# Weight conversions issued one operation at a time, operand reloads in pieces on another queue, and an earlier first output load, in a fused attention, expert and SiLU kernel

## Chip, cores and metric

The kernel runs on one core of a Trainium2 chip. The metric is device time in microseconds (us) from the start to the end of one execution, as the median of several runs. The engines are named as the profile names them: PE multiplies matrices (PEld loads its weights), DVE, ACT and POOL are the vector, scalar and GpSimd engines, and SP only issues DMAs here.

## The reference

Three parts follow each other; only their shapes matter here (8 batches, 8 heads, 576 rows of 64, so 4608 tokens of 512 numbers).

```python
# 1: attention through 32 packed rows per head
p_packed = sm_attn(p, k, v)
x = sm_attn(q, p_packed, p_packed)          # -> (4608, 512)
# 2: one expert of 8 for each token
expert_idx = argmax(normalised(x) @ normalised(expert_emb).T / tau)
out[mask] = gate_w[mask, None] * (relu(x[mask] @ w1[e]) @ w2[e])     # 512 -> 1024 -> 512
# 3: feed forward, with weights that arrive as 64-bit floats
h = out @ w_in                               # 512 -> 2048
y = (h / (1 + exp(-h))) @ w_out              # 2048 -> 512
```

## The kernel before

**Attention** (to about 195 us of the profile) is ordered by a table of start times (`TIMES`) and is not touched.

**The middle stage**, `experts` (195 to 522 us), handles the 8 batches b one after the other. For a batch, `A(m)` for m = 0 to 7 makes the hidden layer: 12 matmuls (L528 to L530), then ACT writes a high part (L533) and DVE the remainder (L537). `Mm` prepares the next batch. Then `Bm(c)` for c = 0 to 3 makes the output columns: 48 matmuls (L602 to L604) that need the high and low part of one block of `w2` (`split_w2`, DVE L575), and `Y` (DVE L613) drains the result. Four PSUM tiles `ps` are used in turn. Beside this, the 64-bit numbers of `w_in` and `w_out` are turned into 32-bit ones: 32 tiles of 512 KB are loaded into two buffers `cin` (`conv_load`), `conv` makes six integer operations of each on DVE (L653 to L658) and the result is stored to `wf_d` (`conv_store`). `todo` and `plan` say how many whole tiles are done after each `Bm(c)`: mostly one, two after `Bm(1)`. The program text sets the order on every engine.

**The last stage**, `ffn`, has two parts. The first (522 to 888 us) makes h and its SiLU in 40 groups. `group(z, g)` takes token block z (512 columns for z = 0 to 3, 256 for z = 4) and weight block g. A group is seven products `Pm` of six matmuls each (L854 to L856), that is 42 matmuls; DVE adds (L847) and ACT applies SiLU (L888); four results go to DRAM (`c_d`, `store`, L898) from a ring `cs` of seven buffers. The seventh product of a group, `last`, runs inside the next group, so a weight operand is free only then. Four calls of `hook(h)` in each group let a list `side` of small jobs run (`later(at, ...)` puts a job there for a time `4 * group + h`). Among these jobs are differences of `w_out` blocks: `o_load` reads two tiles `raw` from `wf_d`, `out_sums` makes four DVE subtractions, `u_store` writes `u_d`. The weight operands (1792 KB each) live in four places TT; the groups of the last sweep (list index 16 to 31 of `order`) need the blocks 4 to 7 again. `t_load` (L1036) reads each back from `t_d` on POOL's queue, right after the group that `next_t` names:

```python
next_t = {19: (4, 0), 20: (5, 1), 21: (6, 2), 23: (7, 3)}
...
        group(z, g)
        if i - 1 in next_t:
            t_load(*next_t[i - 1])
```

The second part (888 us to the end) makes the output in 18 units of seven `product`s with 24 matmuls each (L1142 to L1144). A unit reads four or five pieces of `c_d` (`load_unit`, L1084) into `raws`; `split` makes a high part on ACT (L1113) and a low part on DVE; `drain` adds the products up. The first unit's loads stand before the group with index 30, `t_raw` (the raw weights of two more operands) before group 31 and behind the last one. `x_load` (L1245) brings 7 x 512 KB of `w_out` blocks on POOL's queue at index 29, and `x_build` splits them. `order0` is the order of the seven products in the first unit.

Of the kernel before, what the change touches and what calls it, by code (L numbers as in the profile page):

```python
# [539 lines left out]
def experts(tc, st, sums, R, P, first, ident, a2_d, y_d, g_d, pp_d, w1, w2, win, wout, wf_d, u_d):  # L540
# [106 lines left out]

    def conv(x):
# [4 lines left out]
        DVE.tensor_scalar(out=g, in0=hi, scalar1=-(1 << 31), scalar2=1 << 30, op0=ALU.bitwise_and, op1=ALU.bitwise_or)  # L653
        DVE.tensor_scalar(out=u, in0=hi, scalar1=(1 << 31) - 1, scalar2=None, op0=ALU.bitwise_and)
        DVE.tensor_scalar(out=u.bitcast(F32), in0=u.bitcast(F32), scalar1=EXP_LO, scalar2=EXP_HI, op0=ALU.max, op1=ALU.min)
        DVE.scalar_tensor_tensor(out=g, in0=lo, scalar=29, in1=g, op0=ALU.logical_shift_right, op1=ALU.bitwise_or)
        DVE.tensor_scalar(out=u, in0=u, scalar1=4, scalar2=1, op0=ALU.logical_shift_left, op1=ALU.logical_shift_right)
# [4 lines left out]
        if 7 < i < 16:  # L662
# [9 lines left out]
    def conv_store(x):  # L672
        SP.dma_start(out=wf_d[corder[x]], in_=cout[corder[x]])
# [66 lines left out]
    todo = list(range(32))  # L740
    plan = {(0, 0): 0, (0, 1): 0, **{(b, 1): 2 for b in range(1, 7)}, **{(B - 1, c): 0 for c in range(4)}}
    for b in range(B):
# [27 lines left out]
        for c in range(4):  # L770
# [45 lines left out]
            for x in xs:  # L816
                conv_store(x)


def ffn(tc, st, sums, y_d, wf_d, t_d, c_d, u_d, out):  # L820
# [37 lines left out]
    side, clock = [], [0]  # L858
# [21 lines left out]
    def group(z, g):  # L880
# [208 lines left out]
    order0 = (1, 7, 6, 3, 2, 5, 4)  # L1089
# [56 lines left out]
    def drain(s):  # L1146
# [655 lines left out]
```

## Time and profile before

| what | value |
|---|---|
| median of 3 runs (lowest to highest) | 1269.62 us (1269.46 to 1269.73) |
| the profiled execution's own time | 1268.04 us |
| its span, first to last instruction | 1265.6 us |
| busy: PE, PEld, DVE, ACT, POOL | 1202.6 (95%), 1090.8 (86%), 853.7 (67%), 522.4 (41%), 92.6 us (7%) |
| mean granted clock of TensorE | 0.990 |
| DMA | 256.79 MB, mean 203 GB/s |

The profile is one execution; its time lies 1.58 us below the median of the three runs, and 2.4 us of it lie outside the span. PE is busy for most of the span, so what another engine does costs time only where PE stands idle or runs at a lower clock. In the rows further down, `x<-p,x` means that a tile x is written from tiles p and x, and `<-` behind a wait names what ended it.

### The profile page before, as it was taken

The page shows a single profiled execution, that of the slowest core. Times are in us where ns is not written, and L with a number is a line of the kernel's source. Part 1 is how long each engine was busy: PE and PEld are TensorE (multiplying, and loading weights), DVE is VectorE, ACT ScalarE, POOL GpSimd, SP SyncE. Part 2 cuts the span into 40 slices and gives each one's busy share as a digit, 9 for nine tenths or more (in the row PEclk, how much of TensorE's full clock was granted, in tenths as well). Part 3 has the DMA queues.
Part 4 walks back from the last instruction along what each step waited for, and adds up shares of the span by engine and source line. Part 5 has one row for each costly group of instructions (what it writes and reads, how often), then busy time and mean ns, then how long its engine had stood idle before and what let it go on. Part 6 is the DMA issues. An engine that isn't in the chain of part 4 may idle for free.

```text
span 1265.6 us, 25188 instructions
## 1 busy us (share of the span) xinstructions
PE 1202.6 (95%) x10016; PEld 1090.8 (86%) x10017; DVE 853.7 (67%) x1477; ACT 522.4 (41%) x898; POOL 92.6 (7%) x180
## 2 busy tenths in 40 slices
PE   6899988999999998999999999799799999999998
PEld 4677677999988998878788878689799999999998
DVE  3566567678987884687767676347766567777775
ACT  2666653332333233364444344235533334333332
POOL 3133220002001011100000000001000000000000
PEclk9999999999999999999999999899899999999999
DMA  7888738579877944575866545877864645545351
GB/s 195 246 231 226 240 124 266 189 236 335 272 234 236 328 139 157 193 231 188 323 251 232 200 167 169 320 251 241 234 175 133 182 135 134 144 113 159 99 154 34
DMA packets 249914, 256.79 MB, mean 203 GB/s; under 512 B 34872, under 2 KB 196664, under 8 KB 248768
## 3 DMA queue, kind: packets, MB, share of 16 engines
q1 hardware_dynamic: 241680, 239.40, 60.1%
q0 software_dynamic: 1584, 11.01, 2.5%
q10 hardware_dynamic: 6528, 4.72, 1.2%
q8 instruction: 80, 1.31, 0.4%
q14 instruction: 42, 0.34, 0.1%
HBM read 165.30 MB, written 89.78 MB: 202 GB/s over the span
## 4 chain that ended last, share of the span: by engine, by line
PE 50%; DVE 5%; DMA 4%; issue 2%; ACT 1%; SPq 0%; DVEq 0%; ACTq 0%
PE p L1144 9%; PE p L1143 9%; PE p L1142 9%; PE p L854 6%; PE p L855 6%; PE p L856 6%; DVE x L847 2%; DMA c_d<-x 2%; DMA raw<-wf_d 1%; DVE raw L847 1%; PE ps L604 1%; PE ps L602 1%; PE ps L603 1%; PE ps L528 0%; PE ps L530 0%
## 5 line engine op out<-in xcount | busy, mean ns | idle before, releaser
L888 ACT ACTIVATE x<-x 128x512 f32<-128x512 f32 (+1 forms) x111 | 66.5, 603 | 151.2 <-DVE x L847 148.8
L847 DVE TENSOR_TENSOR x<-p,x 128x512 f32<-128x512 f32 (+1 forms) x132 | 83.4, 643 | 55.8 <-PE p L856 42.7
L604 PE MATMUL ps<-hkm,w2s 128*128 128x288 f32 x384 | 113.7, 296 | 2.7 <-DVE w2s L575 2.7
L602 PE MATMUL ps<-hkm,w2s 128*128 128x288 f32 x384 | 114.9, 299 | 1.2 <-DVE yb L613 1.2
L1142 PE MATMUL p<-x,x 128*128 128x256 f32 x380 | 108.5, 286 | 0.0
L1143 PE MATMUL p<-x,x 128*128 128x256 f32 x380 | 108.4, 285 | 0.0
L603 PE MATMUL ps<-hqm,w2s 128*128 128x288 f32 x320 | 94.2, 294 | 0.0
L602 PEld LDWEIGHTS ps<-hkm,w2s 128*128 128x128 f32 x384 | 72.3, 188 | 8.1 <-DVE hqm L537 4.2
L604 PEld LDWEIGHTS ps<-hkm,w2s 128*128 128x128 f32 x384 | 72.3, 188 | 3.5 <-DVE w2s L575 3.4
L1142 PEld LDWEIGHTS p<-x,x 128*128 128x128 f32 x380 | 74.0, 195 | 0.0
L1143 PEld LDWEIGHTS p<-x,x 128*128 128x128 f32 x380 | 73.9, 195 | 0.0
L1144 PE MATMUL p<-x,x 128*128 128x256 f32 x256 | 73.2, 286 | 0.0
L528 PE MATMUL ps<-at,mh 128*128 128x288 f32 x224 | 66.9, 299 | 5.4 <-PEq L692 3.8
L1144 PE MATMUL p<-x,e 128*128 128x256 f32 x248 | 70.2, 283 | 0.0
L530 PE MATMUL ps<-at,mh 128*128 128x288 f32 x224 | 66.9, 298 | 0.0
L529 PE MATMUL ps<-at,mh 128*128 128x288 f32 x224 | 66.8, 298 | 0.0
L533 ACT ACTIVATE hkm<-ps 128x576 fp32r<-128x576 f32 x42 | 27.1, 650 | 84.9 <-PE ps L530 84.9
L574 ACT CAST w2s<-w2c 128x1024 fp32r<-128x1024 f32 x32 | 33.7, 1054 | 66.7 <-PE ps L603 32.3
L603 PEld LDWEIGHTS ps<-hqm,w2s 128*128 128x128 f32 x320 | 60.0, 188 | 0.0
L847 DVE TENSOR_TENSOR x<-p,y 128x512 f32<-128x512 f32 (+1 forms) x57 | 33.2, 582 | 39.1 <-PE p L856 31.7
L847 DVE TENSOR_TENSOR x<-x,x 128x512 f32<-128x512 f32 (+2 forms) x58 | 49.5, 853 | 14.4 <-ACT x L1113 11.5
L1152 ACT COPY y<-p 128x256 f32<-128x256 f32 x18 | 6.7, 372 | 126.4 <-PE p L1144 126.4
(425 smaller groups left out, 3857.8 us busy)
## 6 DMA issues: line engine op xcount, KB each, us to landing
c_d<-x SPq DMA_DIRECT2D x144, 256.0 KB, 2.3
raww1c<-c_d SPq DMA_DIRECT2D x36, 512.0 KB, 6.8
rawe<-c_d SPq DMA_DIRECT2D x36, 512.0 KB, 7.0
w1c<-in_moe_w_dram SPq DMA_DIRECT2D x32, 512.0 KB, 6.5
w2c<-in_moe_w_dram SPq DMA_DIRECT2D x32, 512.0 KB, 6.9
y_d<-yb SPq DMA_DIRECT2D x36, 288.0 KB, 5.0
raw<-y_d SPq DMA_DIRECT2D x36, 256.0 KB, 4.0
vm<-in_v_dram SPq DMA_DIRECT2D x8, 1024.0 KB, 10.3
```

What stands on the lines that cost most here:

```text
L528: PE.matmul(out=a[:, i, 0:H2], lhsT=mh[0][:, t, f], rhs=at[0][:, t, n], start=t == 0, stop=False)
L530: PE.matmul(out=a[:, i, 0:H2], lhsT=mh[1][:, t, f], rhs=at[0][:, t, n], start=False, stop=t == 1)
L602: PE.matmul(out=a[:, i, 0:H2], lhsT=h[:, k, :], rhs=hT(0, k, n), start=k == 0, stop=False)
L603: PE.matmul(out=a[:, i, 0:H2], lhsT=h[:, k, :], rhs=hT(1, k, n), start=False, stop=False)
L604: PE.matmul(out=a[:, i, 0:H2], lhsT=l[:, k, :], rhs=hT(0, k, n), start=False, stop=k == 7)
L847: eng.tensor_tensor(out=o, in0=x, in1=y, op=op)
L854: PE.matmul(out=o, lhsT=h, rhs=a[0][k][:, 0:n], start=start and k == 0, stop=False, skip_group_check=True)
L855: PE.matmul(out=o, lhsT=h, rhs=a[1][k][:, 0:n], start=False, stop=False, skip_group_check=True)
L856: PE.matmul(out=o, lhsT=l, rhs=a[0][k][:, 0:n], start=False, stop=k == 1, skip_group_check=True)
L1142: PE.matmul(out=o, lhsT=h[:, g], rhs=x[:, 0:256], start=first and g == gs[0], stop=False, skip_group_check=True)
L1143: PE.matmul(out=o, lhsT=h[:, g], rhs=x[:, 256:512], start=False, stop=False, skip_group_check=True)
L1144: PE.matmul(out=o, lhsT=l[:, g], rhs=x[:, 0:256], start=False, stop=stop and g == gs[-1], skip_group_check=True)
```

## The change

1. In `experts`, `conv` becomes a generator that yields after each of its six DVE operations. `some(n)` first issues the stores of finished tiles and then n operations. `quota` gives the number after each `Bm(c)`, and one operation follows each `A(m)` of the batches 1, 2, 5 and 6.
2. In `ffn`, `t_load` reads a quarter of an operand on SP. The sixteen quarters are put at fixed hooks (`timed`). The differences of the `w_out` blocks 3, 4 and 6 start one group later.
3. The first unit's loads and both `t_raw` go to hooks inside the groups with index 29, 30 and 31. `order0` does product 5 ahead of product 2, with the two lines of `drain` that follow from it.

```diff
     def conv(x):
         i = corder[x]
-        t = cin.pop(i).rearrange("p (n u) -> p n u", u=2)
-        lo, hi = t[:, :, 0], t[:, :, 1]
         u, g, o = cu, cg, cos[x % 4]
-        DVE.tensor_scalar(out=g, in0=hi, ...)
+        lo, hi = [cin[i].rearrange("p (n u) -> p n u", u=2)[:, :, n] for n in range(2)]
+        yield DVE.tensor_scalar(out=g, in0=hi, ...)
...
+        stores.append(i)
+        yield
+
+    work = (f for x in range(32) for f in conv(x))
+
+    def some(n):
+        while stores:
+            i = stores.pop(0)
+            SP.dma_start(out=wf_d[i], in_=cout[i])
+        for _ in range(n):
+            next(work, None)
...
-    plan = {(0, 0): 0, (0, 1): 0, **{(b, 1): 2 for b in range(1, 7)}, **{(B - 1, c): 0 for c in range(4)}}
+    quota = [(0, 0, 6, 6), *[(6, 6, 6, 6)] * 2, *[(7, 7, 7, 7)] * 2, (6, 6, 6, 6), (7, 7, 4, 2), (0, 0, 0, 0)]
...
                 A(m)
                 sums.run(steps[m:m + 1])
+                some(b in (1, 2, 5, 6))
...
-            xs = [todo.pop(0) for _ in range(plan.get((b, c), 1))]
-            for x in xs:
-                conv(x)
+            some(quota[b][c])
...
         def hook(h):
             clock[0] = 4 * (turn[0] - 1) + h
+            for f in timed.pop(clock[0], ()):
+                f()
...
-    def t_load(g, x):
+    def t_load(g, x, i):
         held[g] = x
-        POOL.dma_start(out=TT[x][:, 0:3584].bitcast(F32), in_=t_d[g].bitcast(F32))
+        c = slice(896 * i, 896 * i + 896)
+        SP.dma_start(out=TT[x][:, c].bitcast(F32), in_=t_d[g][:, c].bitcast(F32))
...
-    order0 = (1, 7, 6, 3, 2, 5, 4)
+    order0 = (1, 7, 6, 3, 5, 2, 4)
...
-    next_t = {19: (4, 0), 20: (5, 1), 21: (6, 2), 23: (7, 3)}
+    for g, at4 in ((4, (81, 83, 85, 87)), (5, (88, 89, 90, 91)), (6, (93, 95, 97, 98)), (7, (100, 101, 102, 103))):
+        for i, t in enumerate(at4):
+            timed.setdefault(t + 32, []).append(lambda g=g, i=i: t_load(g, g - 4, i))
...
+    def first_load():
+        raws[0] = quarters("w1c")
+        load_unit(0)
+
+    for t, f in ((117, first_load), (121, lambda: t_raw(6)), (125, lambda: t_raw(7))):
+        timed[t + 32] = [f]
...
-                later(now + 4, *out_sums(x), (0, lambda x=x: u_store(x)))
+                later(now + (8 if x in (3, 4, 6) else 4), *out_sums(x), (0, lambda x=x: u_store(x)))
```

A hook time of 81 + 32 = 113 is 4 x 28 + 1, so hook 1 of the 29th group, which has index 20 in `order`.

**Operand loads.** These are POOL's rows before, near the end of its program: the four operand loads (1792 KB each), then the first of the `x_load`s (`x_7209`, `t_7625` and `t_7701` are the TT places of blocks 5, 6 and 7).

```order
L1036 DMA ta<-t_d 128x3584
L1036 DMA x_7209<-t_d 128x3584
L1036 DMA t_7625<-t_d 128x3584
L1036 DMA t_7701<-t_d 128x3584
L1245 DMA x_7206<-wf_d 128x4x256
```

SP's rows before, in the groups with index 20 and 21 (`c_d_89` to `c_d_92` are the four stores of a group with z = 4; `raw` and `u_d` belong to the `w_out` differences):

```order
L898 DMA c_d_91<-x_7212 128x256
L1057 DMA u_d<-raw 128x256 x4
L898 DMA c_d_89<-x_7212 128x256
L898 DMA c_d_92<-x_7212 128x256
L898 DMA c_d_90<-x_7213 128x256
L965 DMA raw<-wf_d 128x512 x2
L898 DMA c_d_91<-x_7213 128x256
L898 DMA c_d_89<-x_7222 128x256
L898 DMA c_d_92<-x_7212 128x256
L898 DMA c_d_90<-x_7212 128x256
```

And the same place on SP with the change:

```order
L903 DMA c_d_91<-x_7212 128x256
L1044 DMA ta<-t_d 128x896
L903 DMA c_d_89<-x_7212 128x256
L903 DMA c_d_92<-x_7212 128x256
L903 DMA c_d_90<-x_7213 128x256
L1044 DMA ta<-t_d 128x896
L972 DMA raw<-wf_d 128x512 x2
L903 DMA c_d_91<-x_7213 128x256
L1044 DMA ta<-t_d 128x896
L1065 DMA u_d<-raw 128x256 x4
L903 DMA c_d_89<-x_7222 128x256
L903 DMA c_d_92<-x_7212 128x256
```

POOL's four rows are gone; quarters of 448 KB stand between the stores, and the four `u_d` stores moved from group 20 to group 21.

**First unit.** SP's rows before, from the load of the first unit's fifth piece (`x_7210<-c_d_78`) on, with the semaphores that each waits for (DMAHW0 to DMAHW7 are those of SP's own DMAs, in turn, so that an issue waits for the DMA eight issues before it):

```order
L1084 DMA x_7210<-c_d_78 128x8x128 [waits DMAHW5_49,DVE_49]
L898 DMA c_d_86<-x_7213 128x512 [waits DMAHW6_49,Activation_49]
L898 DMA c_d_89<-y_3371 128x256 [waits DMAHW7_49,Activation_49]
L898 DMA c_d_92<-y_3372 128x256 [waits DMAHW0_49,Activation_49]
L898 DMA c_d_90<-x_7211 128x256 [waits DMAHW1_49,Activation_49]
L898 DMA c_d_91<-x_7211 128x256 [waits DMAHW2_49,Activation_49]
L898 DMA c_d_89<-x_7211 128x256 [waits DMAHW3_49,Activation_49]
L898 DMA c_d_92<-raw 128x256 [waits DMAHW4_49,Activation_49]
L898 DMA c_d_90<-raw 128x256 [waits DMAHW5_49,Activation_49]
L1084 DMA raww1c<-c_d_74 128x8x128 [waits DMAHW6_49,DMASW0_49,PE_49]
```

And with the change:

```order
L1092 DMA x_7210<-c_d_78 128x8x128 [waits DMAHW5_49,DVE_49]
L903 DMA c_d_86<-x_7213 128x512 [waits DMAHW6_49,Activation_49]
L903 DMA c_d_89<-y_3371 128x256 [waits DMAHW7_49,Activation_49]
L903 DMA c_d_92<-y_3372 128x256 [waits DMAHW0_49,Activation_49]
L903 DMA c_d_90<-x_7211 128x256 [waits DMAHW1_49,Activation_49]
L903 DMA c_d_91<-x_7211 128x256 [waits DMAHW2_49,Activation_49]
L1092 DMA raww1c<-c_d_74 128x8x128 [waits DMAHW3_49,PE_49]
L1092 DMA raww1c<-c_d_76 128x8x128 [waits DMAHW4_49]
L1092 DMA raww1c<-c_d_77 128x8x128 [waits DMAHW5_49]
L1092 DMA raww1c<-c_d_75 128x8x128 [waits DMAHW6_49]
L903 DMA c_d_89<-x_7211 128x256 [waits DMAHW7_49,Activation_49]
```

The four loads moved ahead of three stores, and the third of them waits for the semaphore of the fifth piece's load.

**Conversions.** DVE's rows before, at the end of the hidden layer of batch 1 and behind `Mm`:

```order
L537 SCALAR_TENSOR_TENSOR hqm<-ps_3378,hvm 128x576
L537 SCALAR_TENSOR_TENSOR hqm<-ps_3379,hvm 128x576
L469 TENSOR_TENSOR at_140<-af,at_139 128x1152
L588 TENSOR_TENSOR mh_143<-ps_3376,mh_142 128x1024
L588 TENSOR_TENSOR mh_143<-ps_3377,mh_142 128x1024
L575 TENSOR_TENSOR w2s_3388<-w2c_3384,w2s_3387 128x1024
L653 TENSOR_SCALAR cg<-cin_3394 128x512
```

And with the change:

```order
L659 TENSOR_TENSOR co_3400<-cu,cg 128x512
L537 SCALAR_TENSOR_TENSOR hqm<-ps_3378,hvm 128x576
L654 TENSOR_SCALAR cg<-cin_3395 128x512
L537 SCALAR_TENSOR_TENSOR hqm<-ps_3379,hvm 128x576
L655 TENSOR_SCALAR cu<-cin_3395 128x512
L469 TENSOR_TENSOR at_140<-af,at_139 128x1152
L588 TENSOR_TENSOR mh_143<-ps_3376,mh_142 128x1024
```

One conversion operation now stands behind each remainder L537, and the first tile of the batch is finished before `Mm`.

## Rows read from the trace of the kernel before

**Rows 1.** Waits of PE, whole span: us in total, times, longest us.
```profile
PE p L854 <- DVE y L847: 9.2, 3, 7.5
...
PE ps L604 <- DVE w2s L575: 2.7, 3, 1.9
PE p L1142 <- ACT x L1113: 2.3, 1, 2.3
...
PE p L1144 <- DVE x L847: 1.9, 3, 0.8
...
PE ps L528 <- DVE hvm L537: 1.6, 1, 1.6
...
PE p L1142 <- DVE raw L847: 1.1, 1, 1.1
```

**Rows 2.** PE by windows: stretch, its us, busy (instructions), clock, DMA share, GB/s.
```profile
226.93:239.60 12.67, 12.67 (x98) 1.00 0.30 102
...
776.98:786.49 9.51, 9.51 (x43) 1.00 0.36 139
797.23:802.26 5.03, 5.03 (x44) 1.00 0.97 337
802.27:821.13 18.86, 11.35 (x44) 0.82 0.95 367
...
880.33:888.28 7.95, 6.26 (x50) 1.00 0.93 276
888.29:938.26 49.97, 44.58 (x338) 0.93 0.69 198
938.27:958.42 20.15, 20.15 (x170) 1.00 0.57 157
```

**Rows 3.** DVE's timeline, 803 to 817.5 us: start, us, operation, [idle before].
```profile
811.68 0.43 DVE L847 TENSOR_TENSOR x<-p,x 128x256 f32<-128x256 f32 x1 [7.52 <-DMA c_d<-x]
815.07 0.43 DVE L847 TENSOR_TENSOR raw<-raw 128x256 f32<-128x256 f32 x1 [2.97 <-DMA raw<-wf_d]
815.41 0.69 DVE L847 TENSOR_TENSOR y<-p,y 128x512 f32<-128x512 f32 x1
```

**Rows 4.** The chain that ended last, 790 to 830 us: start, us, what.
```profile
794.79 8.85 DMA c_d<-x
803.66 11.39 DMA raw<-wf_d
...
817.37 0.43 PE p L856
...
829.34 0.24 PE p L855
```

**Rows 5.** DMA, 793 to 816 us: queues (packets, MB, time), issues (KB, us to landing).
```profile
q0 software_dynamic: 432, 5.51, 62.5%
q1 hardware_dynamic: 2358, 2.49, 30.6%
...
c_d<-x SPq DMA_DIRECT2D x11, 128.0 KB, 9.2
```

**Rows 6.** DMA issues of the whole span, from the page.
```profile
c_d<-x SPq DMA_DIRECT2D x144, 256.0 KB, 2.3
raww1c<-c_d SPq DMA_DIRECT2D x36, 512.0 KB, 6.8
```

**Rows 7.** DVE's groups by line and shape, 226 to 480 us: count, busy, mean ns, idle.
```profile
L658 DVE TENSOR_TENSOR co<-cu,cg 128x512 int32<-128x512 int32 x30 | 20.8, 693 | 1.4
...
L537 DVE SCALAR_TENSOR_TENSOR hqm<-ps,hkm 128x576 fp32r<-128x576 f32 x18 | 13.6, 757 | 10.0 <-ACT hkm L533 10.0
```

**Rows 8.** DVE's timeline in batch 4, 377 to 395 us.
```profile
384.12 0.43 DVE L653 TENSOR_SCALAR cg<-cin 128x512 int32<-128x512 int32 x1 [3.86 <-DMA cin<-in_moe_w_in_dram]
```

**Rows 9.** Timelines of ACT and of DVE, 884.2 to 897 us.
```profile
886.74 1.05 ACT L1113 CAST x<-raww1c 128x1024 fp32r<-128x1024 f32 x1 [1.56 <-DMA raww1c<-c_d]
...
887.82 1.23 DVE L847 TENSOR_TENSOR x<-raww1c,x 128x1024 fp32r<-128x1024 f32 x1 [0.40 <-ACT x L1113]
```

More of the change, by code (lines that the diff above doesn't have):

```diff
@@ L646, in conv_load @@
             SP.dma_start(out=cin[i], in_=wout[128 * (i - 16):128 * (i - 15), :])
+    stores = []
     def conv(x):
         i = corder[x]
-        t = cin.pop(i).rearrange("p (n u) -> p n u", u=2)
-        lo, hi = t[:, :, 0], t[:, :, 1]
         u, g, o = cu, cg, cos[x % 4]
[L653 to L657, printed above, removed]
+        lo, hi = [cin[i].rearrange("p (n u) -> p n u", u=2)[:, :, n] for n in range(2)]
+        yield DVE.tensor_scalar(out=g, in0=hi, scalar1=-(1 << 31), scalar2=1 << 30, op0=ALU.bitwise_and, op1=ALU.bitwise_or)
+        yield DVE.tensor_scalar(out=u, in0=hi, scalar1=(1 << 31) - 1, scalar2=None, op0=ALU.bitwise_and)
+        yield DVE.tensor_scalar(out=u.bitcast(F32), in0=u.bitcast(F32), scalar1=EXP_LO, scalar2=EXP_HI, op0=ALU.max, op1=ALU.min)
+        yield DVE.scalar_tensor_tensor(out=g, in0=lo, scalar=29, in1=g, op0=ALU.logical_shift_right, op1=ALU.bitwise_or)
+        yield DVE.tensor_scalar(out=u, in0=u, scalar1=4, scalar2=1, op0=ALU.logical_shift_left, op1=ALU.logical_shift_right)
         DVE.tensor_tensor(out=o, in0=u, in1=g, op=ALU.bitwise_xor)
@@ L670, in conv @@
                 SP.dma_start(out=u_d[i - 8][:, 512 * n:512 * n + 512], in_=four[n])
-    def conv_store(x):
-        SP.dma_start(out=wf_d[corder[x]], in_=cout[corder[x]])
+        stores.append(i)
[7 more added lines that the diff above has]
+            next(work, None)
     load_w1, load_a2, expert = first.load_w1, first.load_a2, first.expert
@@ L738, in experts @@
         SP.dma_start(out=y_d[B - 1, c], in_=zero)
-    todo = list(range(32))
-    plan = {(0, 0): 0, (0, 1): 0, **{(b, 1): 2 for b in range(1, 7)}, **{(B - 1, c): 0 for c in range(4)}}
+    quota = [(0, 0, 6, 6), *[(6, 6, 6, 6)] * 2, *[(7, 7, 7, 7)] * 2, (6, 6, 6, 6), (7, 7, 4, 2), (0, 0, 0, 0)]
     for b in range(B):
@@ L815, in experts @@
             wait = []
-            for x in xs:
-                conv_store(x)
 def ffn(tc, st, sums, y_d, wf_d, t_d, c_d, u_d, out):
@@ L856, in Pm @@
             PE.matmul(out=o, lhsT=l, rhs=a[0][k][:, 0:n], start=False, stop=k == 1, skip_group_check=True)
-    side, clock = [], [0]
+    side, clock, timed = [], [0], {}
     def some(ns):
@@ L1157, in drain @@
             ACT.copy(out=outs[u][0][:, 0:256], in_=a)
+            if u == 0:
+                write(z, r, 0, outs[u][0])
         elif i == 5:
@@ L1162, in drain @@
             tt(DVE, outs[u][0][:, 256:512], d, v[:, n])
-            write(z, r, 0, outs[u][0])
+            if u:
+                write(z, r, 0, outs[u][0])
         if i == 4:
@@ L1303, in ffn @@
         if i == 30:
-            raws[0] = quarters("w1c")
-            load_unit(0)
             later(now + 1, *chain(*[x_build(x) for x in order2[0:3]]))
         if i == 31:
-            t_raw(6)
             later(now, *chain(*[x_build(x) for x in order2[3:5]], split(0), *[x_build(x) for x in order2[5:7]], (None, None)))
         group(z, g)
-        if i - 1 in next_t:
-            t_load(*next_t[i - 1])
     S4 = one.tile([128, 1024], F32, name="x6", tag="x6")
@@ L1318, in ffn @@
     begin(1)
-    t_raw(7)
     load_unit(1)
```

## The prediction

> **What bounds the kernel now.** I read the waits of PE first, since PE is busy 95% of the span and only its gaps and its slow stretches can be won. Apart from attention, which the change leaves alone, they lie in three places [rows 1]: one wait of 7.5 us on DVE in the h part (L854), a handful of 0.8 to 2.3 us where the output part begins (L1142, L1144), and three waits on `w2s` (2.7 us) and one on `hvm` (1.6 us) in the middle stage. Then I read PE by windows, because a gap can also cost clock [rows 2]. A group with z = 3 has 42 matmuls and takes 9.51 us undisturbed (776.98:786.49), a group with z = 4 takes 5.03. The group (3,3), from 802.27, has the same 42 matmuls and takes 18.86 us at a mean clock of 0.82: 9.35 us lost, 7.5 as the gap and the remaining 1.85 at the lower level of the clock (1.2 GHz), where a matmul takes 0.43 instead of 0.24 us [rows 4]. At the start of the output part, 168 matmuls take 20.15 us in steady state, so the first 336 should take 40.3; they take 49.97. The last group with its closing product (48 matmuls) should take 5.03 x 48/42 = 5.75 and takes 7.95. That makes 9.67 + 2.20 = 11.9 us lost there. In the steady state that follows PE never waits.
>
> **Why the 7.5 us wait exists.** DVE works in order. It stood 7.52 us for a `c_d` store whose ring buffer it wanted, then 2.97 us for `raw<-wf_d`, and only then made the addition that PE waited for [rows 3]. The chain gives the same story in DMAs [rows 4]: a store issued at 794.79 landed after 8.85 us, and the `raw` load that SP could issue only then took 11.39 us more. In that stretch stores of 128 KB took 9.2 us [rows 5], while stores of twice the size land in 2.3 us over the whole span [rows 6]. What filled the DMA engines were POOL's operand loads: queue q0 moved 5.51 MB in 432 packets (12.8 KB each) and held 62.5% of the time, SP's queue q1 moved 2.49 MB in 2358 packets (1.1 KB each) in 30.6% [rows 5]. Small packets stood behind large ones.
>
> **The change, part by part.** The sum is made against the profiled execution (1268.04 us, span 1265.6, 2.4 us around it). The median of the three runs is 1.58 us higher; the difference is put on that median.
>
> *Operand loads in quarters on SP: -9.0 us.* Removed: four POOL loads of 1.84 MB, three of which were in flight within 21 us. Added: 16 SP loads of 0.459 MB (128 x 896 x 4 bytes). POOL has nothing else to do there, so its relief is worth nothing. SP's queue gets, over the groups (4,1), (4,2), (3,3), eight quarters (3.67 MB), the stores (8 x 0.131 + 4 x 0.262 = 2.10 MB), four `u_d` stores (0.52) and four `raw` loads (1.05): 7.34 MB in 5.03 + 5.03 + 9.51 = 19.6 us, or 375 GB/s. The DMA engines moved 337 and 367 GB/s there when 95 to 97% busy [rows 2], so the queue runs 0.4 us late by the end, and up to 2.4 us inside (4,2), whose 2.49 MB need 7.4 us at 337. A store then lands within about 2.3 + 2.4 = 4.7 us. A ring buffer comes round after seven stores, 1.75 groups or 8.8 us in groups of 5.03: DVE does not wait. The wait for `raw` goes as well: `out_sums` of block 4 now starts two groups after its loads are issued instead of one. Moving those subtractions costs nothing: they go from (3,3) into (4,3), where DVE has five additions of 0.43 us and these four, 3.9 us of 5.03. Every quarter is issued at least 9.5 us ahead of the group that multiplies with it (the tightest: the last quarter of block 7, with the whole group (3,6) between). I take 9.0 of the 9.35, for a residue at the knee. Bounds: 9.35, and 0 if the DMA engines stay as full as they were.
>
> A rule speaks against it. The Trainium skill, "DMA: Bandwidth & Descriptors", section "Issuing engines are not separate DMA queues", says that DMAs from any engine share the same 16 DMA engines and that another issuer saves only issue time; by it this term would be 0 and the whole 9.35 us stay. The trace bears it out in that q0 and q1 together fill 93% [rows 5]; it does not say what a spread in time is worth.
>
> *First unit's loads and the order of its products: -1.5 us.* Before, the high part of the first `split` waited 1.56 us on ACT for `raww1c`, but DVE behind it only 0.40 us [rows 9], since it still had remainders of 1.2 us to do. So earlier loads are worth 0.4 us. They cannot land much earlier anyway: two of the four can be issued at once, the third waits for the fifth piece's load, which stands behind POOL's `x_load`s as the stores above did. The stores of groups 29 to 31 queue behind that third load; after `small` the ring has 13 buffers for their 12 stores, so nobody waits for them. The product order is worth its wait: before, product 5 was drained directly ahead of product 4, which adds to a bank that this drain reads (1.1 us, L1142 on DVE raw [rows 1]); now product 2 (24 matmuls, 2.9 us) lies between. The remaining waits there, 2.3 (ACT) and 1.9 us, hang on the serial splits of ACT and DVE, which keep their order. Bounds: 0, and -4.0 if the slow clock that these gaps bring (11.9 lost less 6.6 of waits, 1.3 of them a part of the 9.2 [rows 1], is 5.3 us) halves too.
>
> *Conversions one at a time: -0.7 us.* The same 192 operations. Before, two whole tiles after `Bm(1)` made DVE late: the second tile's first operation waited 3.86 us for its `cin` load, queued behind 2.1 MB of `w1`, and the `w2s` part that PE needs came after it [rows 8]. This is the pattern of the three waits of 2.7 us [rows 1]. They lie in the batches 1, 4 and 5. In 1 and 5 only two operations now stand behind that load instead of six, which clears their waits (0.8 us together); in batch 4 four stand behind it, and of 1.9 us about 1.0 stays. Gain 1.7 us. Against it: an operation (at most 0.69 us) behind each `L537` (0.76) [rows 7] makes 1.45 us per A(m), of the 12.67 / 8 = 1.58 us that PE takes [rows 2], which fits with little to spare. But batch 5 begins with a fresh tile whose load is issued only some 4 us earlier, after batch 4's late end; waits for `cin` reached 3.9 us [rows 8], and I charge 1.0 us. The wait on `hvm` (1.6 us, batch 4, raw tiles of the sums) stays, since nothing in its queue is earlier. Bounds: -4.3 (all waits of 2.7 and 1.6 gone) to +3.0.
>
> Sum: -9.0 - 1.5 - 0.7 = -11.2 us. 1268.04 becomes 1256.8 as profiled, and 1269.62 becomes **1258.4 us**.
>
> **Rivals.**
> 1. *The bytes decide, not the queue.* If quarters, stores and `raw` loads together keep the DMA engines as full as POOL's loads did, SP's in-order queue carries the delay to every store, and DVE waits again. For: 375 GB/s asked, 337 to 367 shown, and the skill's rule above. Against: the excess is at most 2.4 us of queue. Half of the 9.35 us kept gives 1258.4 + 4.5 = 1262.9; all of it, which is also the case that the change does not do what it says, 1267.4.
> 2. *Conversions in front of the remainders* (the other side). In A(m), a conversion that waits for its `cin` stands in front of the next `L537`, which PE needs four tiles later. This decides from the point at which a load is later than the slack, three A(m) or 4.7 us. To make the kernel slower, the four batches 1, 2, 5, 6 must lose over 3.4 us each, so loads over 8 us late. For: DVE already waits 3.9 us for `cin` [rows 8]. Against: in batches 1, 2 and 6 the tile is loaded a whole `Bm` ahead. At 3.6 us each it is 1258.4 + 14.4 = 1272.8.
> 3. *The clock comes back too.* With no gap of 7.5 us, and fewer at the output's start, the slow stretches after them shrink: another 2.5 us there and 1 in the middle stage, 1254.9.
>
> **How the numbers follow.** About 0.2% (2.5 us) is what a measurement of this kernel can tell from no change, so faster means below 1267.1. Forecast 0.55 (1256 to 1261); rival 3 0.17; rival 1 0.22 (0.17 of it with a part of the gain, 0.05 with none); rival 2 0.06. Faster 0.55 + 0.17 + 0.17 = 0.89; same 0.05; slower 0.06. The range 1253.0 to 1264.5 takes in the forecast, most of rival 3 (down to -9.4 - 4.0 - 2.7 = -16.1 us) and the nearer half of rival 1, about 0.82.
>
> **What would show it.** Right: the group (3,3) takes 9.5 to 10 us at full clock; no DVE wait on `c_d` over 1 us between 795 and 815; POOL's four `t_d` loads gone and 128 KB stores landing in under 5 us there; the 1.1 us wait on DVE raw gone, the 2.3 us wait on ACT still there; the waits of PE on `w2s` down to about 1 us. Wrong: a PE wait over 3 us on L854 in the last sweep, a new PE wait on `hvm` or `hqm` in batches 1, 2, 5 or 6 with DVE waiting for `cin`, or a wait on `t_d` in front of the groups (3,4) to (3,7).

## The result, and the profile after the change

| | before | after |
|---|---|---|
| median (lowest to highest), us | 1269.54 (1267.97 to 1269.73), 4 runs | 1253.82 (1251.32 to 1258.94), 4 runs |
| profiled execution: its time / its span, us | 1268.04 / 1265.6 | 1251.32 / 1249.6 |

The ratio is 0.9884, with a 95% interval of 0.9851 to 0.9917. The medians differ by 15.7 us, the forecast said 11.2.

PE's windows by stage come first. Columns: stretch, its us, busy (instructions), clock, DMA share, GB/s. The stages are cut at PE's first matmul of the middle stage, of the last stage, and of the output part. Then the output part's first 336 matmuls, and the 72 of them from number 97 on. Before:

```profile
195.36:522.83 327.47, 316.97 (x2472) 0.99 0.72 237
522.83:888.28 365.45, 351.62 (x1680) 0.99 0.67 234
888.29:1265.60 377.31, 367.31 (x3026) 0.99 0.51 140
...
907.16:918.11 10.95, 9.12 (x74) 1.00 0.26 83
```

After, with the group (3,3) as the last row:

```profile
194.15:518.66 324.51, 317.01 (x2472) 0.99 0.71 239
518.66:874.03 355.37, 349.12 (x1680) 1.00 0.71 241
874.04:1249.56 375.52, 365.81 (x3026) 1.00 0.51 140
874.04:922.23 48.19, 43.09 (x338) 0.96 0.69 200
892.54:902.08 9.54, 8.97 (x74) 1.00 0.36 105
797.97:806.90 8.93, 8.93 (x45) 1.00 1.01 324
```

Of the 16.0 us between the two spans, 10.1 were won in the first part of the last stage, 3.0 in the middle stage, 1.8 in the output part, and 1.2 in attention, which the change does not touch. The group (3,3) took 18.86 us at a clock of 0.82 [rows 2]; now it takes 8.93 at full clock and PE never waits in it.

The waits of PE after, whole span (us in total, times, longest), beside [rows 1]:

```profile
PE p L1150 <- ACT x L1121: 3.8, 1, 3.8
...
PE ps L528 <- PEq L701: 2.4, 1, 2.4
PE ps L528 <- DVE hvm L537: 2.2, 2, 1.4
...
PE p L859 <- DVE y L852: 1.6, 2, 1.3
...
PE p L1152 <- DVE x L852: 1.3, 2, 0.8
...
PE ps L604 <- DVE w2s L575: 0.2, 1, 0.2
```

The 7.5 us on DVE y is gone (1.6 remain, elsewhere), w2s fell from 2.7 to 0.2, and the 1.1 on DVE raw is gone. Two waits grew: the one on ACT at the output's start from 2.3 to 3.8 us, and the one on hvm from 1.6 to 2.2, now in two places. The wait on PE's own queue (the branch ahead of the last batch, 3.8 before) is 2.4.

The DMA view after, 789 to 812 us, against [rows 5] (queue: packets, MB, time; then issues: KB each, median us to landing):

```profile
q1 hardware_dynamic: 3893, 6.38, 87.5%
...
c_d<-x SPq DMA_DIRECT2D x11, 128.0 KB, 3.1
```

POOL's queue q0 has no row any more, SP's moves the quarters, and a 128 KB store lands in 3.1 us instead of 9.2. Both are medians over eleven stores, some of which left while no operand load was in flight; the next section takes them apart.

### The profile page after: what moved, and what is told of

It is laid out like the page before. It is cut to its first block, busy times and chain, and to the rows that moved or that the text cites. A ratio compares the mean times of both kernels' runs of the same rounds, so it can differ in the third digit from the quotient of the medians.

```text
span 1249.6 us, 25196 instructions
## 1 busy us (share of the span) xinstructions
PE 1199.0 (96%) x10016; PEld 1088.1 (87%) x10017; DVE 855.3 (68%) x1477; ACT 522.7 (42%) x898; POOL 92.7 (7%) x176
## 4 chain that ended last, share of the span: by engine, by line
PE 53%; DVE 4%; DMA 2%; issue 2%; ACT 1%; SPq 0%; DVEq 0%; ACTq 0%
PE p L1152 10%; PE p L1151 10%; PE p L1150 10%; PE p L859 7%; PE p L861 7%; PE p L860 7%; DVE x L852 2%; DVE raw L852 1%; DMA c_d<-x 1%; PE ps L604 1%; PE ps L603 1%; PE ps L602 1%; PE ps L528 0%; PE ps L529 0%; PE ps L530 0%
```

## Experiments

The stages of every profile, cut as above (us; each is one execution). The stage that an edit is about is in bold; in the rows named "before", everything else is as before, and in all others as after the change.

| kernel | attention | middle stage | last stage, first part | output part | 336 matmuls |
|---|---|---|---|---|---|
| before | 195.36 | 327.47 | 365.45 | 377.31 | 49.98 |
| after | 194.15 | 324.51 | 355.37 | 375.52 | 48.19 |
| before, loads on SP | 195.25 | 328.54 | **355.76** | 377.42 | 50.36 |
| before, later differences | 193.71 | 326.91 | **359.26** | 377.70 | 50.33 |
| quarters on POOL | 197.35 | 327.03 | **357.20** | 375.72 | 48.36 |
| whole loads on SP | 195.30 | 323.29 | **357.25** | 375.67 | 48.62 |
| differences not later | 195.15 | 326.83 | **355.41** | 376.04 | 48.71 |
| old product order | 194.76 | 324.83 | 355.14 | **378.11** | **50.31** |
| first loads at old place | 192.53 | 327.18 | 355.14 | **376.72** | **49.39** |
| old conversions | 196.28 | **325.72** | 355.28 | 376.62 | 48.92 |
| none behind A(m) | 193.16 | **330.58** | 356.85 | 375.52 | 48.19 |
| 2 builds on POOL | 197.11 | **323.96** | 355.23 | **375.33** | **47.87** |
| 4 builds on POOL | 192.76 | **324.73** | 354.58 | **377.80** | **50.47** |
| w_out loads on SP | 198.58 | **324.76** | **357.89** | **377.24** | **49.57** |

### The last sweep: queue, pieces or order?

The change did three things here: another queue, four pieces spread over time, and later differences of the `w_out` blocks. My theory was that the spread counts.

**Quarters on POOL**, the rest as changed:

```diff
-        SP.dma_start(out=TT[x][:, c].bitcast(F32), in_=t_d[g][:, c].bitcast(F32))
+        POOL.dma_start(out=TT[x][:, c].bitcast(F32), in_=t_d[g][:, c].bitcast(F32))
```

> The changed kernel with one edit: the sixteen quarters of the operand loads are issued on POOL instead of SP, at the same hooks. Theory (the spread in time cures the wait): the queue does not matter, the group (3,3) takes 8.9 to 10 us as with the change (8.93), the 128 KB c_d stores land in a median of 3 to 5 us, no PE wait over 1 us there, time 1250 to 1256 us. Rival (POOL's queue itself delays SP's small packets): the DVE wait on a c_d store returns in part, 128 KB stores land in 6 us or more, (3,3) takes 12 us or more, time 1256 us or more.

Measured: 1259.05 us. The DMA view, 789 to 812 us, and the window of the group (4,3), behind (3,3) (busy of PE, PEld, DVE, ACT, POOL; clock, DMA share, GB/s):

```profile
q0 software_dynamic: 827, 4.78, 56.4%
...
c_d<-x SPq DMA_DIRECT2D x9, 128.0 KB, 7.5
```

```profile
812.57:820.12 7.55, 5.94 (x43) 5.48 (x42) 3.96 (x10) 2.43 (x5) 0.00 (x0) 1.00 0.86 310
```

The stores were slow again, 7.5 us, with the same pieces at the same hooks. (3,3) kept its 8.93 us, but (4,3) took 7.55 instead of 5.7, with PE idle for 1.6. So this cut does not bring quick stores while the quarters are on POOL. It does not show what a spread in time is worth, since the quarters were hardly spread here. POOL issues a load as soon as PE is done with its place; SP has stores ahead of it in its order. POOL's rows for block 4 here, and the first and the last of SP's after:

```profile
793.91 0.71 POOL L1044 DMA_DIRECT2D ta<-t_d  x1 [262.82 <-PE p L861]
795.36 1.61 POOL L1044 DMA_DIRECT2D ta<-t_d  x3 [0.73 <-PE p L861]
```

```profile
790.89 0.38 SPq L1044 DMA_DIRECT2D ta<-t_d  x1
...
802.08 0.32 SPq L1044 DMA_DIRECT2D ta<-t_d  x1
```

On POOL the four left 9.7 to 7.2 us ahead of (3,3), which begins at 803.64; on SP from 7.1 us ahead of it (797.97) to 4.1 behind. The rival's price was too high; of the 7.7 us by which this profile is longer than that of the change only 1.8 lie in this stage.

**Whole loads on SP**, where they stood before, the rest as changed:

```diff
-        c = slice(896 * i, 896 * i + 896)
-        SP.dma_start(out=TT[x][:, c].bitcast(F32), in_=t_d[g][:, c].bitcast(F32))
+        SP.dma_start(out=TT[x][:, 0:3584].bitcast(F32), in_=t_d[g].bitcast(F32))
...
-    for g, at4 in ((4, (81, 83, 85, 87)), (5, (88, 89, 90, 91)), (6, (93, 95, 97, 98)), (7, (100, 101, 102, 103))):
+    next_t = {19: (4, 0), 20: (5, 1), 21: (6, 2), 23: (7, 3)}
...
         group(z, g)
+        if i - 1 in next_t:
+            t_load(*next_t[i - 1])
```

> The changed kernel with whole operand loads (1792 KB) on SP, issued behind the groups with index 20, 21, 22 and 24 as before the change. Theory (the spread cures it): each load is 1.84 MB at 337 GB/s = 5.4 us in front of the stores that follow it on the queue, so 128 KB stores land in 8 us or more, DVE waits for the ring again and the group (3,3) takes 13 to 19 us; time 1256 to 1264 us. Rival (it is the queue: SP's own order keeps the packets fair): (3,3) stays under 10 us, time 1250 to 1256 us.

Measured: 1253.27 us. The DMA view, 789 to 812 us:

```profile
c_d<-x SPq DMA_DIRECT2D x11, 128.0 KB, 2.7
...
c_d<-x SPq DMA_DIRECT2D x4, 256.0 KB, 9.2
```

The rival's time, with (3,3) at 8.92 us. But the 2.7 us is mostly that of stores that left with no load in flight. The one 128 KB store that was issued behind a load and whose landing the trace tells (796.23) took 8.4 us, as the theory said of such stores; DVE waited 3.0 us for a store, and PE not at all in (3,3). The 256 KB stores of (3,3) were late too (9.2 us), and one group later PE waited 1.1 us on ACT. The stage took 1.9 us more than with quarters.

**Differences not later**, the rest as changed:

```diff
-                later(now + (8 if x in (3, 4, 6) else 4), *out_sums(x), (0, lambda x=x: u_store(x)))
+                later(now + 4, *out_sums(x), (0, lambda x=x: u_store(x)))
```

> The changed kernel, but the differences of the w_out blocks 3, 4 and 6 begin one group after their loads are issued, as before the change. Theory (the raw loads land in 4.5 us with the quarters, and a group takes 5.03): DVE waits at most 1 us for raw, PE at most 0.5 us, the group (3,3) takes 8.9 to 9.6 us, time within 1 us of the changed kernel in this stretch. Rival (the shift is needed): DVE waits 2 to 3 us for raw<-wf_d, PE 1.5 us or more in (3,3) or (4,3).

Measured: 1255.18 us, the stage 355.41 against 355.37: with the quarters on SP the later differences are worth nothing.

**Later differences alone**, on the kernel before:

```diff
-                later(now + 4, *out_sums(x), (0, lambda x=x: u_store(x)))
+                later(now + (8 if x in (3, 4, 6) else 4), *out_sums(x), (0, lambda x=x: u_store(x)))
```

> The kernel before with one edit: the differences of the w_out blocks 3, 4 and 6 begin one group later; the operand loads stay whole and on POOL. Theory (two waits in a row on DVE, 7.52 us for a c_d store and 2.97 us for raw): the second goes, the first stays, the longest PE wait falls from 7.5 to 4 to 6 us, the group (3,3) takes 15 to 17.5 us instead of 18.9, time 1265 to 1268 us. Rival (the raw wait alone made it): the PE wait falls under 2 us, (3,3) under 12 us, time 1262 us or less. Second rival (nothing: the store's wait alone makes the PE wait): (3,3) stays at 18.5 to 19 us.

Measured: 1260.02 us. The DMA view, 793 to 816 us, and the waits of PE, 793 to 835 us:

```profile
c_d<-x SPq DMA_DIRECT2D x8, 128.0 KB, 7.6
```

```profile
PE p L854 <- ACT x L927: 2.1, 1, 2.1
```

PE's window of (4,3), behind (3,3):

```profile
808.86:818.42 9.56, 7.44 (x43) 0.82 0.89 327
```

The stores stayed slow, yet (3,3) took 8.93 us. What remained of the loss lies in (4,3), which took 9.56 us instead of 5.7: 2.1 us of idle time, and behind it 3.4 us at the lower level of the clock (0.50 from 814.19 to 817.61). But for 0.1 us of that wait these are the first rival's numbers: 6.2 us of the loss go with the place of three blocks' differences (four subtractions and four `u_d` stores each). So I read [rows 3] wrongly, as two waits of which one would stay: the wait for `raw` went, and the longest wait of DVE for a store fell from 7.5 to 3.1 us with it. Whether it is the subtractions ahead of PE's addition on DVE, or the `u_d` stores ahead of the ring's stores on SP, was not tried apart.

**Loads on SP alone**, on the kernel before; one word:

```diff
-        POOL.dma_start(out=TT[x][:, 0:3584].bitcast(F32), in_=t_d[g].bitcast(F32))
+        SP.dma_start(out=TT[x][:, 0:3584].bitcast(F32), in_=t_d[g].bitcast(F32))
```

> The kernel before with one word changed: the whole operand loads (1792 KB) are issued on SP instead of POOL, at the same places; nothing is cut, spread or shifted. Stretch to read: from the first matmul of the first part of the last stage to the first product (365.5 us before, 355.4 with the whole change, 359.3 with the shift of the differences alone, 357.2 with whole loads on SP and the shift). Theory (SP's packets get a smaller share while POOL's loads are in flight, and this goes when one queue carries both): 128 KB c_d stores land in under 5 us (9.2 before), the 7.5 us wait shrinks below 3 us, the stretch takes 356 to 360 us. Rival (cutting and spreading is needed when the differences are not shifted): the wait stays at 5 us or more and the stretch takes 361 us or more. By the Trainium skill's rule that DMAs of any engine share the same 16 DMA engines (DMA: Bandwidth & Descriptors), the stretch would stay at 365 us.

Measured: 1258.77 us. The DMA view, 793 to 816 us, and PE's windows of the stage and of (3,3):

```profile
c_d<-x SPq DMA_DIRECT2D x11, 128.0 KB, 2.7
```

```profile
523.79:879.55 355.76, 349.48 (x1680) 1.00 0.69 240
...
803.08:812.40 9.32, 9.21 (x44) 1.00 1.02 383
```

That one word wins 9.7 of the stage's 10.1 us, better than the theory's range (356 to 360), with nothing cut and no line moved. DVE's wait for `raw` is still there (2.7 us, 3.0 before), and the group takes 9.32 us against 8.93. (With the later differences added, the run of whole loads above took 1.5 us more; each is one profile.)

But the word moves the loads in time as well. POOL's first two loads before, and SP's here:

```profile
794.11 0.71 POOL L1036 DMA_DIRECT2D ta<-t_d  x1 [264.54 <-PE p L856]
799.15 0.55 POOL L1036 DMA_DIRECT2D x<-t_d  x1 [4.33 <-PE p L856]
```

```profile
799.96 0.40 SPq L1036 DMA_DIRECT2D ta<-t_d  x1
...
804.82 0.39 SPq L1036 DMA_DIRECT2D x<-t_d  x1
```

Measured from the start of (3,3) (802.27 and 803.08), the first two leave 5.0 and 4.9 us later, and the third 11.0 us. Nor is 2.7 us the time of a store beside a load: six of the eleven stores had left before the first load. These are the landings (shortest, median, longest) of the `c_d` stores that were issued with a load in flight, before (794.7 to 812 us) and here (801.4 to 804.6):

```profile
DMA to landing us min/median/max: 5.3/11.3/16.0
```

```profile
DMA to landing us min/median/max: 6.2/7.2/8.0
```

Directly behind a whole load a store took about the same on either queue: 8.9 and 8.6 us (before, and with later differences alone) with the load on POOL, 8.0 and 8.4 us with it on SP. The longest, 14.1 to 16.0 us, are three stores that left before POOL's second load (797.46 to 798.53, the load at 799.15) and landed behind it; here the two stores ahead of the second load (803.92 and 804.33, the load at 804.82) took 6.4 and 6.2 us and landed 4 us before it. So the traces show a difference of order: in this stretch no load on SP passed an earlier store. Which of the two wins the 9.7 us, the queue itself or the later times, no run separates; one with the loads on POOL, held back to SP's times, would.

The Trainium skill, "DMA: Bandwidth & Descriptors", section "Issuing engines are not separate DMA queues", says that another issuing engine saves only the time of the issue; by that the stage would have stayed at 365 us. It did not, but as the loads also left later, the run does not tell whether that rule fails here. The same page, section "Queues, rings and completion order", has each DMA engine take turns between queues by whole packets. That fits in kind, since a packet of q0 held 12.8 KB and one of q1 1.1 KB before [rows 5]; but with quarters on POOL a packet of q0 held 4.78 MB / 827 = 5.8 KB and the stores still took 7.5 us. Why a POOL load passes a store is left open.

### The output part

**Old product order**, the rest as changed (the two lines of `drain` go back as well):

```diff
-    order0 = (1, 7, 6, 3, 5, 2, 4)
+    order0 = (1, 7, 6, 3, 2, 5, 4)
```

> The changed kernel with the old order of the first unit's products (2 ahead of 5) and the old place of one output store. Theory (the swap is worth its wait): the PE wait of 1.07 us on DVE raw in front of product 4 returns; the output part (first product to the end, 375.5 us with the change, 377.3 before) takes 376.5 to 376.9 us. Rival (the swap also gives back the second slow stretch of the clock, 1.7 us): the output part takes 377.0 us or more, with two stretches of 3.4 us at the lower level of the clock. Second rival (nothing): under 376.0 us.

Measured: 1254.6 us. The waits of PE, whole span, and its window over the matmuls 97 to 168 of the output part:

```profile
PE p L1150 <- DVE raw L852: 1.1, 1, 1.1
```

```profile
893.93:904.88 10.95, 9.12 (x74) 1.00 0.23 74
```

The wait came back, and these 72 matmuls take 10.95 us, as before the change (10.95), against 9.54. That is the worth of the swap: 1.4 us. The output part as a whole took 378.1, in the rival's range, but not by the rival's cause: the clock of the first 336 matmuls was 0.93 here, and also 0.93 in five other profiles with the changed output part, which took 48.19 to 48.92 us (mean 48.56) where the change took 48.19 at 0.96. The second slow stretch is worth some 0.4 us, not 1.7. The rest of the 2.6 us lies in the first 96 matmuls (19.2 against 18.5; 18.5 to 19.2 in five other runs with the same code there) and behind the last.

**First loads at the old place**, the rest as changed:

```diff
-    for t, f in ((117, first_load), (121, lambda: t_raw(6)), (125, lambda: t_raw(7))):
-        timed[t + 32] = [f]
...
         if i == 30:
+            first_load()
...
         if i == 31:
+            t_raw(6)
...
     begin(1)
+    t_raw(7)
     load_unit(1)
```

> The changed kernel with the first unit's loads and both t_raw at their old places (in front of the groups with index 30 and 31, and behind the last). Theory (DVE's serial chain of builds and splits sets the start, not the loads): the first wait on ACT stays at 3.8 us, product 1 starts at most 0.5 us later against the last group, output part 375.5 to 376.1 us. Rival (the loads set the start): the wait on ACT grows by 1 us or more and the output part takes 376.5 us or more.

Measured: 1253.33 us. PE's window over the first 96 matmuls:

```profile
874.85:894.54 19.69, 14.69 (x97) 0.83 1.07 307
```

Between the two: the wait on ACT stayed at 3.8 us, as the theory said, but a wait of 0.8 us for the low part of the first split came ahead of it, and the 96 matmuls took 19.7 us against 18.5 to 19.2. That makes the earlier loads worth 0.9 us (19.69 less the mean 18.8 of six runs). But the three profiles of the kernel before with its old loads took 18.87, 19.23 and 19.24 us there, only 0.3 more than that mean, so 0.3 to 0.9 us is all that can be said.

The wait of 3.8 us hangs on this. ACT's timeline after, 878.5 to 880.3 us (start, us, operation, [idle before]):

```profile
878.91 0.42 ACT L893 ACTIVATE x<-x 128x256 f32<-128x256 f32 x1 [1.63 <-DVE x L852]
879.23 1.03 ACT L1121 CAST x<-raww1c 128x1024 fp32r<-128x1024 f32 x1
```

The high part that PE's 3.8 us wait is for (879.23) stands behind the last SiLU, and this behind DVE's builds. Before, the same wait was 2.3 us: product 0 then ran at the lower level of the clock (0.50 from 889.06 to 892.47, 1.2 GHz) and ended later. In the two other profiles with the old output part, where the clock fell behind product 0, the wait is 3.8 us too. From the first matmul to the end of this wait it is 6.8 us before, 6.6 in those two and 6.3 after, so the chain nearly kept its length.

### The middle stage

**Old conversions**, the rest as changed: `conv`, `plan` and `conv_store` as before, in place of

```diff
-    quota = [(0, 0, 6, 6), *[(6, 6, 6, 6)] * 2, *[(7, 7, 7, 7)] * 2, (6, 6, 6, 6), (7, 7, 4, 2), (0, 0, 0, 0)]
...
-                some(b in (1, 2, 5, 6))
```

> The changed kernel with the old conversions (whole tiles). Theory (single operations clear the three w2s waits of 2.7 us and bring a new wait on hvm of 0.8 to 2.1 us in batch 5; the rest is variation from run to run): the waits of 0.2 to 0.4, 1.5 to 1.9 and 0.4 us on w2s return, the one on hvm in batch 5 goes, the middle stage (327.5 before; 323.3 to 327.0 us in four runs of the new conversions) takes 325.5 to 327.5 us. Rival (the conversions give 3 us, as the two first profiles read): 327 us or more here, and below 325 us in the other runs of this series. The wait on the branch ahead of the last batch (3.8 before, 2.0 to 2.6 with the change): 3.1 us or more here if it goes with the conversions, 2.0 to 2.6 us if not.

Measured: 1255.89 us. The waits of PE, whole span:

```profile
PE ps L528 <- PEq L692: 3.4, 1, 3.4
...
PE ps L604 <- DVE w2s L575: 2.5, 4, 1.4
```

As the theory said: w2s waits of 2.5 us return, the hvm wait of batch 5 goes (1.5 us stay in batch 4), and the stage took 325.72. Over all profiles with the changed conversions and nothing else changed in this stage it took 323.29 to 327.18 us, mean 325.6 of six; with the old ones 325.72 to 328.54, mean 327.2 of four. The difference, 1.6 us, is smaller than the spread of either. The wait at the branch goes with the conversions: 3.1 to 3.8 us in four runs with the old ones, 1.8 to 2.8 in ten with the new. Why was not tried.

The new wait in batch 5 shows in DVE's timeline after, 399 to 402 us:

```profile
399.74 0.43 DVE L654 TENSOR_SCALAR cg<-cin 128x512 int32<-128x512 int32 x1 [2.48 <-DMA cin<-in_moe_w_in_dram]
400.08 0.75 DVE L537 SCALAR_TENSOR_TENSOR hvm<-ps,hkm 128x576 fp32r<-128x576 f32 x1
```

A conversion waits 2.48 us for its tile, and the remainder that PE wants stands behind it. PE loses 0.8 us to 2.1 us there (six runs).

**No conversions behind A(m)**, the rest as changed:

```diff
-                some(b in (1, 2, 5, 6))
...
-    quota = [(0, 0, 6, 6), *[(6, 6, 6, 6)] * 2, *[(7, 7, 7, 7)] * 2, (6, 6, 6, 6), (7, 7, 4, 2), (0, 0, 0, 0)]
+    quota = [(0, 0, 6, 6), *[(8, 8, 8, 8)] * 2, *[(7, 7, 7, 7)] * 2, (8, 8, 8, 8), (9, 9, 6, 4), (0, 0, 0, 0)]
```

> The changed kernel without the conversions behind each A(m); the batches 1, 2, 5 and 6 do two more after each Bm(c). Theory (in batch 5 the operation behind A(m) waits for a cin tile loaded late and holds up the remainder behind it): the hvm wait in batch 5 (0.8 to 2.1 us) goes, the w2s waits stay under 0.8 us in total, the middle stage takes 322.5 to 325 us. Rival (the operations behind A(m) are what clears the w2s waits): w2s waits of 1.5 us or more return in total, the stage takes 325 us or more.

Measured: 1257.97 us. The waits of PE, whole span:

```profile
PE ps L528 <- DVE yb L613: 3.7, 4, 1.6
PE ps L604 <- DVE w2s L575: 3.2, 6, 1.2
...
PE ps L528 <- DVE hvm L537: 2.0, 1, 2.0
```

PE's window of the first 336 matmuls of the output part (for the clock, above):

```profile
880.59:928.78 48.19, 43.38 (x338) 0.93 0.69 198
```

The theory fell. The hvm wait in batch 5 went, but the stage took 330.58 us, 5.0 over the mean of the change: two more operations behind each Bm(c) bring 3.2 us of w2s waits and 3.7 us on `yb` (the drain of the last Bm that the next A(m) needs the PSUM tile of). So in this one profile the single operations are worth nothing without the places behind A(m); the cut matters because it lets them be used.

This profile also shows a sign that the prediction had called wrong: in the last stage, which is as after the change, PE waited 1.3 us (to 847.39) for a quarter of an operand, `t<-t_d`. SP had issued it at 842.10, 4 us before the wait began, where the prediction counted on at least 9.5 us ahead of the group. No other profile has this wait.

### Three attempts to do better

**Two builds on POOL**, and the late tiles of batch 4 and 5 out of the way:

```diff
+        if x in ("T1", "T4"):
+            return put(d, d[:, :, 256:512].bitcast(F32))[0], lambda: tt(POOL, d[:, :, 256:512], d[:, :, 256:512].bitcast(F32), d[:, :, 0:256].bitcast(F32), ALU.subtract)
...
-                some(b in (1, 2, 5, 6))
+                some(b in (1, 2, 6) or b == 5 and m > 3)
...
-    quota = [(0, 0, 6, 6), *[(6, 6, 6, 6)] * 2, *[(7, 7, 7, 7)] * 2, (6, 6, 6, 6), (7, 7, 4, 2), (0, 0, 0, 0)]
+    quota = [(0, 0, 6, 6), *[(6, 6, 6, 6)] * 2, *[(7, 7, 7, 7)] * 3, (7, 7, 4, 2), (0, 0, 0, 0)]
...
-            if b in (2, 3) and c == 2:
+            if b in (2, 3) and c == 0:
```

> The changed kernel with three edits: the low parts of T1 and T4 of the w_out blocks (2 DVE operations of 1.22 us at the start of the output part) go to POOL; no conversion behind the first four A(m) of batch 5, these four behind its Bm(c); the raw loads of the sums of batches 3 and 4 two Bm earlier. Theory (DVE's serial chain sets the start of the output part; hvm waits come from late loads): the PE wait of 3.8 us on ACT falls to 1.0 to 1.8 us, the hvm waits of 1.4 to 1.9 us (batch 4) and 0.8 to 2.1 us (batch 5) go, in all 3 to 5.5 us faster than the changed kernel, 1248 to 1251 us. Rival (the waits only move: PE waits later for the next splits and w2s): within 1 us of the changed kernel. Other side (POOL's operation of 4096 bytes per partition takes 4 us or more and slows DVE beside it): slower by 1 to 3 us at the output's start.

Measured: 1253.44 us (1250.57 to 1254.31, 4 runs), ratio to before 0.9871 (0.9828 to 0.9914): no difference from the change's 0.9884 that can be measured. The waits of PE, whole span:

```profile
PE p L1152 <- DVE x L852: 2.7, 2, 2.2
PE ps L528 <- DVE yb L613: 2.3, 2, 1.7
...
PE p L1150 <- ACT x L1121: 2.1, 1, 2.1
```

The waits moved, as the rival said: the one on ACT fell from 3.8 to 2.1 us, the next, on DVE x, rose from 0.8 to 2.2; the hvm waits went and 2.3 us on `yb` came. 336 matmuls took 47.87 us, 0.3 less.

**Four builds on POOL**: the same with `("B22", "B21", "T1", "T4")`.

> As e8_pool_builds, with the low parts of B22 and B21 on POOL too (4 operations in all). Theory (DVE's chain): another 1 to 2.4 us faster than e8_pool_builds, the wait of 1.3 us ahead of the last closing product goes too. Rival (POOL's four operations in a row of 4 us each come too late for product 4, which needs B22): a new PE wait of 2 us or more on POOL, slower than e8_pool_builds.

Measured: 1255.96 us (1251.62 to 1256.94, 4 runs), ratio 0.9898 (0.9857 to 0.9940); 336 matmuls 50.47 us, 2.6 more than with two. The timelines of DVE and of POOL, 868 to 882 us:

```profile
872.67 3.30 DVE L852 TENSOR_TENSOR raww1c<-x,raww1c 128x1024 f32<-128x1024 f32 x1
...
878.97 2.60 DVE L852 TENSOR_TENSOR x<-raww1c,x 128x1024 fp32r<-128x1024 f32 x1 [2.34 <-ACT x L1121]
```

```profile
869.15 11.34 POOL L852 TENSOR_TENSOR x<-x 128x1024 fp32r<-128x1024 f32 x4 [13.96 <-ACT x L1229]
```

Not the rival's cause: PE did not wait on POOL. It is rather the other side that was named for two builds: DVE's operations beside POOL's took 3.30 and 2.60 us instead of 1.23.

**w_out loads on SP**, with the middle stage's edits of the last two:

```diff
-        POOL.dma_start(out=XX[:, :, i + 256:i + 512].bitcast(F32), in_=w_out(x, slice(1, 5)))
+        SP.dma_start(out=XX[:, :, i + 256:i + 512].bitcast(F32), in_=w_out(x, slice(1, 5)))
```

> The changed kernel with two edits: the seven loads of w_out blocks (512 KB each, POOL's last queue entries, in flight while 128 KB c_d stores take 8.7 to 12.3 us) are issued on SP too; and the edit of e8_pool_builds in the middle stage (no conversion behind the first four A(m) of batch 5, earlier raw loads of the sums). Theory (stores beside POOL loads are slow wherever they meet, but here nobody waits for them): 128 KB stores of that stretch land in 3 to 6 us, yet the first 336 matmuls of the output part still take 48.0 to 48.9 us (48.2 with the change) and the wait on ACT stays at 3.8 us, since DVE's chain of builds and splits sets the start; the middle stage takes 323.5 to 325 us; median 1250 to 1254 us. Rival (the loads of the first unit and the w_out blocks set the start): the wait on ACT falls by 1 us or more, the 336 matmuls take under 47.5 us. Other side: SP stands at a load that waits for PE, and the stores behind it hold up DVE or PE ahead of the output part: the first part of the last stage takes 356 us or more (355.4).

Measured: 1258.43 us (1254.17 to 1260.25, 5 runs), ratio 0.9899 (0.9881 to 0.9916). A wait of PE that is now there twice:

```profile
PE p L1150 <- ACT x L1121: 4.4, 2, 2.3
```

The other side's time came true, though not for its reason: SP waited only 0.3 us for PE ahead of the seven loads. But SP issues in order and spent 862.58 to 870.65 us on them, and the first unit's loads behind them were issued 9.0 us ahead of the first product instead of 12.1. PE waited 2.1 us for the first product and 1.4 us more in the 336 matmuls. The queue that won 9.7 us in the last sweep loses 3.9 here (357.89 + 49.57 against 355.37 + 48.19), where nobody waited for the stores.

None of these is shown to beat the change.

## Why the prediction was right, and where its steps failed

**Operand loads, forecast -9.0, measured -10.1.** The size was off by the base: I took 9.51 us for an undisturbed group with z = 3, but one that follows a group with z = 4 takes 8.93 (797.97 to 806.90 after), since it runs that group's last product, of half the columns, in place of its own. So 9.9 us were there to win, and no residue stayed. The delay of a store held: 4.7 us forecast, 2.4 to 4.9 for the 128 KB stores that left beside quarters (793.7 to 804.3 after). What failed is the step from there to the gain. The sum rested on quarters spread over the hooks; whole loads on SP at their old lines give 9.7 of the 10.1 us, although stores behind such a load took 6.2 to 8.4 us. And it took the waits for the store and for `raw` as two in a row; moving the differences alone gives 6.2 us, and together with quarters on POOL 8.25. The parts do not add up, since each removes the same wait of PE. So the size of this term, right as it is, bears out that the wait goes and not why. "Small packets stood behind large ones" is not shown: directly behind a load the queue made little difference (8.9 and 8.6 us against 8.0 and 8.4).

**Rival 1, the bytes decide,** fell: the DMA engines stayed as busy (share 1.01 in (3,3), 0.95 before [rows 2]), PE did not wait, and DVE waited for no DMA. Full engines alone did not make the wait.

**First unit and product order, forecast -1.5, measured -1.6.** (375.85 us, the mean of the six profiles with both edits and nothing else new in the output part, against 377.48, the mean of the three with neither.) Within it the swap was worth 1.4 instead of 1.1, and the earlier loads 0.3 to 0.9 against 0.4; only the lower end fits the sum. That the 2.3 us wait on ACT stays held; that it would grow to 3.8 I did not see.

**Conversions, forecast -0.7, measured -1.6 on the means, within the spread of single runs.** The w2s waits fell to 0.2 to 1.3 us in total (forecast 1.0), the late tile of batch 5 costs 0.8 to 2.1 (forecast 1.0), and the hvm wait of batch 4 stayed (1.4 to 1.9). Not foreseen: 1 us less at the branch. So the direction fits, but the runs do not settle the size. **Rival 2** fell for the batches 1, 2 and 6 and holds in small for batch 5.

**Rival 3, the clock,** named the nearest number (1254.9) for a wrong reason: the slow stretch in the last sweep went, but that was in the forecast; at the output's start one stretch of 3.4 us more or less was worth 0.4 us on the mean (48.19 us at 0.96, 48.56 at 0.93).

The three measured parts sum to -13.3 us, inside the interval of the ratio (0.9851 to 0.9917 is -18.9 to -10.5 us). The remaining 2.4 us of the medians are no more than runs differ in parts that no edit touches: attention took 192.5 to 198.6 us over the 14 profiles.

## What to carry to other kernels

Before cutting and spreading a transfer that delays small stores, issue it unchanged on the stores' own queue and look: here one word gave 9.7 of 10.1 us. Look in the trace at when the transfer now leaves, since another queue is also another order, and at the stores one by one, since a median mixes those beside the transfer with those far from it. Do so only where the transfer's own wait holds nothing up, since on an in-order queue what stands behind it waits as well. And where several edits remove one wait, price the wait once: each alone may win most of it, and the sum of the parts misleads.

## What the hardware showed that I had not expected

- A 128 KB store that was issued with operand loads in flight took 5.3 to 16.0 us beside whole loads on POOL (before), 4.1 to 13.3 us beside quarters on POOL, 6.2 to 8.4 us beside whole loads on SP (two runs) and 2.4 to 4.9 us beside quarters on SP (after). On POOL a later load landed ahead of earlier stores; on SP the stores landed first.
- A subtraction of 128 x 1024 on DVE took up to 3.30 us beside POOL's of the same shape, 1.23 alone [rows 9]; POOL's took 2.8 on average (11.34 / 4). In the run with two builds a subtraction on DVE that began 0.3 us ahead of POOL's kept its 1.23 us, and POOL's took 3.15. The Trainium skill, "GPSIMD Engine Reference", section "1. Specifications", says that GpSimd shares its SBUF interfaces with VectorE, in contention when an instruction of the latter has two SBUF inputs; these have two, and the traces agree.
- A stretch of 3.4 us at the lower level of the clock, of which half would be lost if PE alone set the pace, cost 0 to 0.7 us at the output's start (five profiles at 0.93 against one at 0.96): there PE waits for DVE and ACT, and part of the slow time is time that it would have waited.
